# The first phase of a concatenated S4D and attention kernel on one Trainium2 core: its instructions in the order of a list scheduler, seeds of 544 columns, negated factors made in the loop, scaling by dt inside the transposing matmuls

## The chip, the core and the metric

The kernel runs on one core of a Trainium2 chip. The core has five engines with a queue of instructions each: TensorE (PE in the profile; PEld is its load of the stationary operand), VectorE (DVE), ScalarE (ACT), GpSimd (POOL) and SyncE (SP), which here issues nearly all transfers between the device's memory, SBUF and back. Matmuls write to PSUM, of which the kernel uses eight banks of 128 x 512 float32. An engine executes its queue in order; an instruction waits until the semaphores it names have been raised.

The metric is the device time of one execution in microseconds (us). The kernel before takes 1304.7 us, the median of three runs (1302.42 to 1306.85).

## The reference

Two results stand side by side in the output, 2048 x 448 each, in float32.

The first is a diagonal state-space layer (S4D) with D = 448 channels and N = 256 states: its kernel is a sum of 256 complex exponentials, which is then convolved with the input by FFT.

```python
dt = jnp.exp(log_dt)
A = -jnp.exp(log_A_real) + 1j * A_imag
C = (C_real + 1j * C_imag) * dt[:, None]
P = jnp.exp((A * dt[:, None])[:, :, None] * pos[None, None, :])
K = 2.0 * jnp.einsum("dn,dnl->dl", C, P).real
...
y = jnp.fft.irfft(Uf * Kf[None, :, :], L2)[:, :, :L]
return y + u * D_skip[None, None, :]
```

The second is softmax attention with 16 heads of 28 over 2048 positions.

```python
qkv = (x @ wqkv).reshape(B, S, 3, H, Dh)
scores = jnp.einsum("bhqd,bhkd->bhqk", q, k) * Dh ** -0.5
o = jnp.einsum("bhqk,bhkd->bhqd", softmax(scores), v)
return o.transpose(...).reshape(B, S, D) @ wo
```

## The kernel before

`body` has a first phase, a loop and a tail.

**First phase** (the block `with ExitStack() as st`). Two kinds of work run beside each other.

*Projections.* The input x is worked on in four chunks of 512 positions. `transposes` turns a chunk on PE (64 transposes in all) and splits it into a high part `xh` (ACT) and a low part `xl` (DVE). The weights are split in the same way into `w_g` (for queries and keys, kept in the tile that later holds the first keys, `k0_t`) and `vh`, `vl` (for values); ACT makes the high parts, DVE the low parts of `w_g`, POOL those of the values. `qk_proj` makes the queries (s = 0) or keys (s = 1) of one of four head groups for one chunk with 12 matmuls of 512 columns; `v_proj` makes the values of 128 positions with 12 matmuls of 448 columns. In all that is 32 x 12 and 16 x 12 matmuls. The function `evac` that each of them returns splits a result into `hl` (two buffers), by ACT and DVE, and SP stores it to memory (`k_d`, `q_d`, `v_d`); for the first two chunks of keys a difference of two halves, `kd_d`, is stored as well. `project` emits one projection and, behind it, the `evac` of the one before.

*Seeds.* The exponentials are not computed one by one. For each of eight groups of 56 channels, `seeds` makes a few powers of each state's factor (exponentials and sines on ACT, phases reduced on DVE, products on POOL), from which the loop later builds all others by doubling. A group's seeds are 672 columns: 256 for `e` (eight powers of it, the 0th being the constants 1 and 0), 128 for `g` and 288 for `F_Z`, six factors in three forms, namely real part, negated imaginary part and imaginary part. `times_dt` scales four inputs by dt on ACT, then `turn` transposes them on PE. SP stores the seeds to `sd_d` in two parts (`put_e`, `put_g`).

The work is listed in 41 slots (`n_stage`): projections are spread over the first `PW` = 37, the stages of the seeds follow at an offset per group, and `ahead` puts early loads at given slots (`A0`, `A1`, `KW`). In this phase `nc.kept` is empty, and the framework's own scheduler sets the order of the instructions on each engine.

*The first maxima.* The softmax subtracts the exact maximum of each row. One unit of the attention is one head group and one chunk of queries; there are 16 units. For unit 0 the maxima over all keys are made at the end of the first phase, after all projections: the pools of the projections are closed, `load_k(0, j, ...)` has brought the four heads' keys (khat, 16 loads of 256 KB; they lie where the weights lay), and 16 groups of five matmuls follow, with one Relu of 1024 columns on ACT and one combined add and maximum of 1024 columns on DVE per group. `max_end` turns the result and `max_put` stores it into the queries' tile with two small transfers issued by ACT. The loop's first scores need it.

**Loop** (256 steps, `NS`). From here on the written order is kept on all engines. A step handles 128 keys of one unit: four score matmuls (`s_mm`, results `pss`, three banks) whose exponential ACT writes to `p`, four matmuls `po<-p,v`, and four matmuls (`pm`) that prepare the next unit's maxima with DVE's reductions. Between them the step takes pieces of the S4D part: `k_seeds` copies the seeds of one of 56 blocks of eight channels from the loaded tile `sdb` into `e` and `g` on ACT, `e_power` doubles `e` with nine products and sums on POOL, `g_powers` does the same for `g` on DVE from a copy `zg` of the factors (`k_start`), `k_mm` multiplies both on PE, and other jobs (`u_stage1`, `u_stage2`, `spectrum`, `finish`) do the transforms. A block is due every `KP` = 3.5 steps.

**Tail.** After the last blocks, the rest of the spectra, the last unit and the output projection.

Matmuls of float32 operands show in the profile as two or four instructions each; queries, keys and projections use a one-pass type and show as one. All instructions that are issued through the wrapper class `Kept` carry one line number, L76, so groups are told apart by their tiles.

Of the kernel before, what the change touches and what calls it, by code (L numbers as in the profile page):

```python
# [8 lines left out]
F32 = mybir.dt.float32  # L9
# [8 lines left out]
L = 2048  # L18
# [25 lines left out]
A0, A1, KW = 26, 34, (33, 35, 36)  # L44
# [13 lines left out]
F_G = 256  # L58
F_Z = F_G + 128
SDF = F_Z + 18 * 16  # L60
# [5 lines left out]
class Kept:  # L66
# [5 lines left out]
    def __getattr__(self, name):  # L72
        f = getattr(self.engine, name)

        def call(*args, **kw):
            i = f(*args, **kw)  # L76
            return self.owner.tc.keep_in_program_order(i) if self.name in self.owner.kept else i
# [3 lines left out]
class Engines:  # L81
    def __init__(self, tc):
        self.tc, self.kept = tc, ()
# [4 lines left out]
KEPT = {"p": (), "a": ("tensor", "vector", "scalar", "gpsimd", "sync"), "f": ()}  # L88
# [3 lines left out]
def body(ctx, tc, a, out):  # L92
# [41 lines left out]
    k0_p = pool(k0_st, "k0_p", side="right")  # L134
    k0_t = k0_p.tile([128, HG, L], F32R, name="khat")
# [10 lines left out]
    def load_k(g, j, p):  # L146
        if j == 0:
            t = k0_t if g == 0 else p.tile([128, HG, L], F32R, name="khat")
            kt_g[g] = [t[:, i] for i in range(HG)]
# [49 lines left out]
    def max_end(u, ps):  # L199
        nc.tensor.transpose(ps[:16, :128], m_u[u, 1], ident)  # L200
        mh = q_p.tile([16, 2, 128], F32R, name="mh")
# [11 lines left out]
    with ExitStack() as st:  # L213
        sst, xst, wst, mst, psx, psm = (ExitStack() for _ in range(6))
# [3 lines left out]
        y_p = pool(wst, "y_p", side="right")  # L218
        ps_w[0] = pool(psx, "ps_w", 1, PSUM)
# [3 lines left out]

        xns = {}

        def load_x(c):
            xs = x[c * CQ:(c + 1) * CQ, :].rearrange("(t p) d -> p t d", p=128)
            for h in range(2):
                xns[c, h] = y_p.tile([128, 2, D], F32, name="xn", bufs=3)
# [3 lines left out]
        w_g = k0_t[:CK].rearrange("p g (i s k h e) -> p i s k g h e", i=2, s=2, k=NCK, h=HG)  # L233
        vh = y_p.tile([CK, NCK, D], F32R, name="vh")
        vl = y_p.tile([CK, NCK, D], F32R, name="vl")
        nc.gpsimd.memset(k0_t[:CK].rearrange("p g (n e) -> p (g n) e", e=32)[:, :, DH:].bitcast(F32), 0.0)
        vst = [v_p.tile([128, NK // NQ, HG, 32], F32, name="v", bufs=5).rearrange("p t h e -> p (t h) e") for _ in range(2)]
        for t in vst:
            nc.gpsimd.memset(t[:, :, DH:DH + 1], 1.0)
            nc.gpsimd.memset(t[:, :, DH + 1:], 0.0)  # L240
        wns = []
        for i in range(2):
            wn = t_p.tile([128, 3, LV, BO * 16], F32, name="tri", bufs=2).rearrange("p t k h -> p (t k h)")
# [9 lines left out]
        def load_nat(o):  # L253
            nats[o] = s_p.tile([PO, 4, 256], F32, name="nat", bufs=2)
# [4 lines left out]
        dt_all = s_p.tile([PO, 5, NO], F32, name="dt_all")  # L259
# [12 lines left out]
        for k in range(NCK):  # L272
            for s in (1, 0):
# [3 lines left out]
                nc.vector.tensor_tensor(lo, src, hi.bitcast(F32), ALU.subtract)  # L277
# [27 lines left out]
        def turn_dt():  # L305
            dt_ps = ps_t.tile([128, CQ], F32, name="pt")[:PO, :NO]
            nc.tensor.transpose(dt_ps, dt_o, ident[:NO, :NO])
            for i, f in enumerate((1.0, 0.15915494309189535, 2.0, -2.0, -1.0)):
                nc.vector.tensor_scalar(dt_all[:, i, :], dt_ps, f, None, op0=ALU.mult)

# [3 lines left out]
        def seeds(o):  # L314
# [9 lines left out]
            def times_dt(i):  # L324
# [833 lines left out]
```

## Time and profile before

| | |
|---|---|
| median of three runs | 1304.7 us |
| profiled execution, device time | 1307.74 us |
| its span, first to last instruction | 1305.7 us |
| PE busy in the span | 1228.7 us (94%), 12193 matmul instructions |
| DVE, ACT, POOL busy | 907.0 us (69%), 980.3 us (75%), 865.9 us (66%) |
| moved by DMA | 205.28 MB, mean 157 GB/s |
| mean granted TensorE clock | 0.976 |

The profiled execution is one run of its own; its device time is about 2 us above its span and 3.0 us above the median of the three.

A row of a table by stretch gives the stretch, its length, the busy time and number of instructions of PE, PEld, DVE, ACT and POOL, the granted TensorE clock as a share of full speed, the mean busy share of the 16 DMA engines and the rate in GB/s. A row of a group gives line, engine, operation, output tile and input tiles, shapes and count, then busy time and the mean duration in ns, then the idle time of the engine just ahead of these instructions and what ended it. A row of the timeline gives start and duration. Matmuls overlap one another in the records: one of 0.40 us can follow the last after 0.23 us.

### The profile page before, as it was taken

What the parts mean: (1) busy time and instruction counts of PE and PEld (TensorE: products, weight loads), DVE (VectorE), ACT (ScalarE), POOL (GpSimd) and SP (SyncE); (2) the same over time, 40 slices, a digit from 0 to 9 for tenths busy, and PEclk for the clock granted to TensorE, in tenths of its full rate; (3) what the DMA queues carried; (4) which work ended last, traced back from release to release, by engine and by line L of the source; (5) the groups of instructions that cost most, each with busy time, mean ns of one, the idle gap of its engine ahead of it and who ended that gap; (6) DMA issues with size and microseconds to landing.
All of it is one profiled execution on the core that took longest, in us unless ns stands there. A gap on an engine that the chain in (4) does not pass through costs nothing.

```text
span 1305.7 us, 32148 instructions
## 1 busy us (share of the span) xinstructions
PE 1228.7 (94%) x12193; PEld 695.7 (53%) x12193; DVE 907.0 (69%) x2001; ACT 980.3 (75%) x2046; POOL 865.9 (66%) x684
## 2 busy tenths in 40 slices
PE   6888877799999999999999999999997999999998
PEld 5766755355555555555555555555554555545333
DVE  5676656677777787777788888888986555636111
ACT  4877875588888888888788888888886666756463
POOL 2677654478888788888769999999995221424421
PEclk9989887799999999999999999999999999999999
DMA  6677679735866455468634232743324453647666
GB/s 202 207 273 257 218 259 271 212 66 136 185 147 142 109 149 157 142 169 231 162 104 105 56 83 62 157 111 78 82 59 139 146 158 136 203 142 238 202 161 175
DMA packets 200082, 205.28 MB, mean 157 GB/s; under 512 B 95992, under 2 KB 158520, under 8 KB 197880
## 3 DMA queue, kind: packets, MB, share of 16 engines
q1 hardware_dynamic: 199864, 203.22, 56.1%
q8 instruction: 96, 1.57, 0.5%
q14 instruction: 58, 0.48, 0.1%
q10 hardware_dynamic: 64, 0.02, 0.0%
HBM read 120.74 MB, written 82.18 MB: 155 GB/s over the span
## 4 chain that ended last, share of the span: by engine, by line
PE 72%; POOL 8%; ACT 7%; DVE 5%; DMA 4%; issue 4%; SPq 0%; ACTq 0%; POOLq 0%
PE pm L76 39%; PE pss L76 16%; PE po L76 16%; POOL sg L76 2%; POOL e L76 2%; DMA khat<-k 2%; POOL tri L76 2%; ACT tri L76 1%; ACT sg L76 1%; DVE mx L76 1%; POOL p L76 1%; ACT L76 1%; ACT p L76 1%; POOL eu L76 1%; DVE rl L76 1%
## 5 line engine op out<-in xcount | busy, mean ns | idle before, releaser
L76 ACT ACTIVATE p<-pss 128x512 f32<-128x512 f32 x1024 | 560.4, 609 | 109.9 <-PE pss L76 105.9
L76 PE MATMUL pss<-qhat,khat 128*128 128x512 f32 x1024 | 405.7, 402 | 4.0 <-DMA qhat<-mh 2.2
L76 DVE TENSOR_REDUCE mx<-pm 128x1 f32<-128x512 f32 x480 | 308.3, 683 | 121.2 <-PE pm L76 119.5
L76 PE MATMUL pm<-khat,qhat 128*128 128x512 f32 x720 | 314.4, 437 | 6.1 <-ACT rl L76 3.5
L76 POOL TENSOR_TENSOR e<-e,sdb 128x256 f32<-128x256 f32 x168 | 202.0, 1203 | 108.7 <-ACT e L76 67.2
L76 PE MATMUL po<-p,v 128*32 128x512 f32 x2048 | 271.0, 597 | 0.0
L76 POOL TENSOR_TENSOR e<-e,eu 128x256 f32<-128x256 f32 x168 | 248.3, 1478 | 13.2
L76 PEld LDWEIGHTS pm<-khat,qhat 128*128 128x128 f32 x720 | 135.4, 188 | 206.4 <-ACT p L76 47.0
L76 PEld LDWEIGHTS pss<-qhat,khat 128*128 128x128 f32 x1024 | 191.2, 189 | 52.5 <-ACT p L76 13.8
L76 DVE CUSTOM_DVE_ANT_0 rl<-pm,rl 128x512 f32<-128x512 f32 x240 | 165.3, 689 | 70.0 <-ACT rl L76 67.7
L76 POOL TENSOR_TENSOR eu<-e,sdb 128x256 f32<-128x256 f32 x168 | 202.3, 1204 | 0.0
L76 POOL TENSOR_TENSOR p<-pr,pr 64x448 f32<-64x448 f32 x64 | 73.2, 1144 | 155.6 <-PE pm L76 122.3
L76 DVE TENSOR_TENSOR g<-g,zg 128x128 f32<-128x128 f32 x392 | 162.0, 413 | 3.6
L76 ACT ACTIVATE rl<-pm 128x512 f32<-128x512 f32 x240 | 145.3, 605 | 7.7 <-issue 4.1
L76 PE MATMUL pm<-xh,khat 112*128 112x512 f32 x256 | 89.7, 431 | 19.6 <-DVE hl L76 10.6
L76 PE MATMUL pm<-kdif,qhat 128*128 128x512 f32 x240 | 97.0, 404 | 1.7 <-DVE pr L76 1.1
L76 DVE TENSOR_TENSOR zg<-g,zg 128x128 f32<-128x128 f32 x224 | 88.0, 393 | 5.3
L76 PEld LDWEIGHTS pm<-e,g 128*32 128x32 f32 x3584 | 56.9, 110 | 49.2 <-issue 15.7
L76 PE MATMUL pm<-e,g 128*32 128x64 f32 x3584 | 73.6, 223 | 8.7 <-POOL e L76 8.7
L76 ACT ACTIVATE y<-pm 128x448 f32<-128x448 f32 x48 | 26.5, 553 | 59.7 <-PE pm L76 39.1
L76 PEld LDWEIGHTS pm<-xh,khat 112*128 112x128 f32 x256 | 51.0, 205 | 35.9 <-DVE hl L76 12.6
L76 DVE TENSOR_TENSOR pr<-pm,ub 128x448 f32<-128x448 f32 x64 | 37.0, 619 | 46.9 <-PE pm L76 37.7
(133 smaller groups left out, 1491.6 us busy)
## 6 DMA issues: line engine op xcount, KB each, us to landing
sdb<-sd SPq DMA_DIRECT2D x56, 336.0 KB
khat<-k SPq DMA_DIRECT2D x64, 256.0 KB
qhat<-q SPq DMA_DIRECT2D x64, 256.0 KB
sd<-sg SPq DMA_DIRECT2D x8, 1456.0 KB
k<-hl SPq DMA_DIRECT2D x16, 512.0 KB
q<-hl SPq DMA_DIRECT2D x16, 512.0 KB
v<-v SPq DMA_DIRECT2D x32, 256.0 KB
mw<-in_mw SPq DMA_DIRECT2D x16, 512.0 KB
```

Of the source, the lines that this page charges most:

```text
L76: i = f(*args, **kw)
```

## The change

- **Order of the first phase.** The instructions of the phase are no longer emitted at once but collected by a new class `Plan`, each with an assumed duration, the tiles it reads and writes and a tag (p for projections, s for seeds, m for maxima). `Plan.order` is a list scheduler: it computes for each instruction the longest chain behind it, and then repeatedly takes, for the engine that is free first, the ready instruction with the longest chain (chains of seeds are weighted). The instructions are emitted in that order, which is then kept on all five engines. So that the plan can tell buffers apart, the tiles of a ring are allocated once and taken in turn (`ring`).
- **First maxima inside the phase.** The groups of unit 0 are part of the plan. The weights move to a tile of their own, so that the first keys' tile takes the place of the values' weights and the input's tiles (`change`), and is loaded once those are done. The last chunk's work starts with the keys of head group 0, then its four value projections, then the other seven projections. Each group's work is in two halves of 512 columns: 32 Relus and 32 combined maxima. The projections get three buffers of one pool (`pm_r`), shared with the maxima.
- **Splitting the weights.** The low parts of `w_g` are made on POOL instead of DVE.
- **Seeds of 544 columns.** The 0th power of `e` is no longer stored (224 columns), but set once in the loop's two `e` tiles; of the three forms of a factor, two are stored (192 columns). In the loop ACT makes the negated form of 96 columns for each of the 56 blocks, into the tail of `sdb`; the products read the two imaginary forms in reverse order.
- **Scaling by dt.** Three of the four inputs are no longer scaled by ACT; instead their transposes become matmuls with an identity scaled by dt (`dg`, made once on POOL). The factor 2 moves into the constant `wb`.
- **Smaller edits.** One exponential over all 15 powers in place of two instructions; one copy of `g` in place of four; a negation in `g_base` moves from ACT to POOL.

The diff, cut to its core:

```diff
-A0, A1, KW = 26, 34, (33, 35, 36)
+A0, A1 = 18, 28
+MG = {41: (2, ()), 42: (3, ()), 43: (0, (8, 9)), 44: (1, (10, 11)), 45: (None, (12, 13)), 46: (None, (14, 15)), 47: (None, (0, 1)),
+      48: (None, (2, 3)), 49: (None, (4, 5)), 50: (None, (6, 7))}
-F_G = 256
+F_G = 14 * 16
 F_Z = F_G + 128
-SDF = F_Z + 18 * 16
+SDF = F_Z + 12 * 16
+SDN = SDF + 6 * 16
...
+            if self.owner.plan is not None:
+                return self.owner.plan.add(self.name, name, f, args, kw)
...
-KEPT = {"p": (), ...
+KEPT = {"p": ("tensor", "vector", "scalar", "gpsimd", "sync"), ...
...
+    def order(self):
+        for o in reversed(self.ops):
+            k = o.tag, o.engine
+            tail[o.i] = max([cost(o) + self.GAP + tail[j] for j in after[o.i]] + [o.span + chain.get(k, 0.0), cost(o)])
...
+        while len(out) < n:
+            e = min((e for e in pools if pools[e]), key=lambda e: max(free[e], min(ready[i] for i in pools[e])))
+            t = max(free[e], min(ready[i] for i in pools[e]))
+            best = max((i for i in pools[e] if ready[i] <= t + 1e-9),
+                       key=lambda i: tail[i] * self.SCALE[self.ops[i].tag] + self.BIAS[self.ops[i].tag] - ...)
...
-                nc.vector.tensor_tensor(lo, src, hi.bitcast(F32), ALU.subtract)
+                nc.gpsimd.tensor_tensor(lo, src, hi.bitcast(F32), ALU.subtract)
...
+            for i in range(2):
+                nc.gpsimd.tensor_tensor(dg[:, i], ident[:PO, None, :PO].to_broadcast([PO, NO, PO]),
+                                        dt_all[:, i, :, None].to_broadcast([PO, NO, PO]), ALU.mult)
...
-                        nc.tensor.transpose(ps[:, i, :, h, :], q["nat"][:, i, h * 128:(h + 1) * 128], ident[:PO, :PO])
+                        if i == 1:
+                            nc.tensor.transpose(ps[:, i, :, h, :], n, ident[:PO, :PO])
+                        else:
+                            nc.tensor.matmul(ps[:, i, :, h, :], n, dg[:, int(i != 2), o].rearrange("p (b e) -> p b e", e=8), start=True, stop=True)
...
-            jobs = v_jobs + jobs if c == NQ - 1 else jobs + v_jobs
+            jobs = jobs[:1] + v_jobs + jobs[1:] if c == NQ - 1 else jobs + v_jobs
...
+        def max_group(i):
+            for h in range(2):
+                pd, pb = pt_r(), pm_r()
+                if h == 0:
+                    mm(pd, q, kd_g[0, j], start=True, stop=True)
+                    mm(pb.rearrange("p (c n) -> p c n", c=2), q, k_late(j, CQ, ...), start=True, stop=True)
+                else:
+                    mm(pd, q, quarter(2), start=True, stop=False)
+                    mm(pd, Late(("nq", j), 128, lambda: nqs[j][:, ts]), quarter(3), start=False, stop=True)
+                    mm(pb, q, quarter(3), start=True, stop=True)
+                rl = rl_r()
+                nc.scalar.activation(rl, pd, AF.Relu)
+                nc.vector.tensor_tensor_reduce(rl, pb, rl, 1.0, -3.0e38, ALU.add, ALU.max, m_u[0][:, j, t, h:h + 1])
...
+        nc.plan = None
+        plan.run()
...
-            es[b] = e = g_p.tile([128, 2, 16, N2], F32, name="e", bufs=2)
-            nc.scalar.activation(e[:, :, :, :8], sds[b][:, :F_G].rearrange("p (c e h) -> p c h e", c=2, e=8), AF.Copy)
+            es[b] = e = e_t[b % 2]
+            nc.scalar.activation(e[:, :, :, 1:8], sds[b][:, :F_G].rearrange("p (c e h) -> p c h e", c=2, e=7), AF.Copy)
+            nc.scalar.activation(sds[b][:, SDF:], sds[b][:, SDF - 96:SDF], AF.Copy, scale=-1.0)
```

More of the change, by code (lines that the diff above doesn't have):

```diff
@@ L213, in body @@
     with ExitStack() as st:
-        sst, xst, wst, mst, psx, psm = (ExitStack() for _ in range(6))
+        sst, xst, wst, yst, psx = (ExitStack() for _ in range(5))
+        k0 = []
         t_p = pool(sst, "t_p")
@@ L505, in body @@
         slots[1].insert(0, turn_dt)
-        pend, n_work = [], len(work)
+        n_work = len(work)
         ahead = collections.defaultdict(list)
```

392 lines of the change are left out of this document (280 added, 112 removed).

## The prediction

> **What bounds the kernel now.** I read the table of busy time by stretch first, to see where an engine is short of work.
>
> ```profile
> 0.00:40.00 40.00, 29.07 (x125) 21.51 (x125) 24.38 (x54) 21.52 (x45) 11.96 (x24) 1.00 0.64 194
> 40.00:180.00 140.00, 122.64 (x544) 97.52 (x544) 93.68 (x139) 107.78 (x183) 97.21 (x67) 0.94 0.74 249
> 180.00:243.00 63.00, 39.87 (x123) 27.18 (x123) 37.12 (x64) 34.07 (x44) 20.83 (x17) 0.77 0.92 262
> 243.00:650.00 407.00, 402.90 (x4497) 215.75 (x4500) 315.61 (x746) 341.32 (x770) 332.41 (x261) 0.99 0.60 150
> 650.00:980.00 330.00, 326.95 (x3803) 183.29 (x3795) 287.52 (x688) 285.10 (x636) 302.01 (x237) 1.00 0.38 91
> 980.00:1306.00 326.00, 307.31 (x3111) 150.49 (x3111) 148.69 (x313) 190.49 (x371) 101.47 (x81) 0.99 0.56 170
> ```
>
> After the stretch and its length come busy time and instructions of PE, PEld, DVE, ACT and POOL, then the granted clock, the DMA share and GB/s. From 243 us on PE is busy 99% of the time up to 980: the attention loop is PE's. Up to 243 us, the first phase, no engine is full, and PE least of all at its end: 544 matmuls in 140 us (3.9 per us), then 123 in 63 us (2.0 per us). So the change is decided in the first phase, and above all after 180 us. The chain of waits there, in order of time:
>
> ```profile
> 208.44 9.86 DMA khat<-k
> 218.32 10.46 DMA khat<-k
> ...
> 236.38 5.56 DMA qhat<-mh
> ```
>
> Two loads of the first keys hold the end for 20 us, then come the last maxima and the 5.56 us store of the maxima into the queries. PE in that stretch, by group, and single rows of the timeline (start, duration):
>
> ```profile
> L76 PE MATMUL p<-khat,qhat 128*128 128x512 f32 x48 | 19.2, 466 | 1.2 <-DMA khat<-k 1.2
> L76 PE MATMUL pm<-xh,khat 112*128 112x512 f32 x24 | 10.4, 524 | 8.0 <-DVE hl L76 8.0
> L76 PE MATMUL p<-kdif,qhat 128*128 128x512 f32 x16 | 7.6, 473 | 7.8 <-DVE hl L76 7.1 <-ACT rl L76 0.7
> L76 PE MATMUL p<-khat,nq 128*128 128x512 f32 x16 | 7.1, 454 | 0.0
> L76 PE MATMUL pm<-xl,khat 112*128 112x512 f32 x12 | 6.1, 504 | 0.0
> ```
> ```profile
> 191.22 0.39 PE L76 MATMUL pm<-xl,khat 112*128 112x512 f32 x1
> ...
> 191.92 0.40 PE L76 MATMUL pm<-xl,khat 112*128 112x512 f32 x1
> ...
> 195.75 0.73 PE L76 MATMUL pm<-xh,khat 112*128 112x512 f32 x2 [2.73 <-DVE hl L76]
> ...
> 197.51 0.63 PE L76 MATMUL pm<-xl,khat 112*128 112x512 f32 x1
> ...
> 198.79 0.63 PE L76 MATMUL pm<-xl,khat 112*128 112x512 f32 x1
> ...
> 233.28 0.73 PE L76 MATMUL p<-khat,qhat 128*128 128x512 f32 x2
> ...
> 242.89 0.77 PE L76 MATMUL pss<-qhat,khat 128*128 128x512 f32 x1 [2.18 <-DMA qhat<-mh]
> ```
>
> Three projections (36 matmuls) and the 80 matmuls of the first unit's maxima run here. From one xl row to the next lie three matmuls: 0.70 us before the gap at 195.75, so 0.233 us each, and 1.28 us after it, so 0.427. At 0.233 the 116 matmuls are 27 us of work in a stretch of 63. PE ends the last maximum at 234.0; the loop's first scores (pss) start at 242.89, 8.9 us later.
>
> **The change part by part.** *The order.* The last chunk's keys of head group 0 are now projected first, then its values, and the first keys' 16 loads stand in SP's queue among the last seven projections' stores. The 80 matmuls stand between those projections on PE. All five engines follow one written order. The 16 loads of kd, four of q and four of the second unit's q also move ahead of stores on SP. So the question is at what rate PE gets through what is left. I count from 40 us. Of the 544 + 123 matmuls, about 6 belong to the loop already: 661. At the middle stretch's 140/544 = 0.257 us each that is 170 us. The later ones are longer than the middle's mean, which holds 88 small transposes, here by group for 40 to 180 us:
>
> ```profile
> L76 PE MATMUL pt<-ident,xn 128*112 128x128 f32 x40 | 6.0, 279 | 1.9 <-DVE xl L76 1.9
> L76 PE MATMUL pn<-ident,nat 56*128 56x56 f32 x48 | 4.2, 228 | 0.0
> ```
>
> If these cost nothing, a middle matmul would be 456/544 x 0.233 = 0.195 us of full-rate work, if they cost as much as the others 0.233; I take 0.203. For the end's 116 at 0.233 that adds 116 x 0.03 x 0.257/0.203 = 4 us, so 174 us, at a granted clock of 0.94. If the gaps that cost clock go, 174 x 0.94 = 164. Bounds: the whole stretch as it ran before, 234 - 40 = 194 us, and 661 x 0.208 (545 at 0.203, 116 at 0.233) at full rate without a gap, 138 us; with 5% gaps 145. I take 163, near the one with full clock, because the order fills the waits for hl (8.0 and 7.1 us above) with other matmuls.
>
> The Trainium skill, "TensorE: Matmul & The Clock Gate", Part 1, says that PE falls to half clock after an idle window of about 3.4 us and needs such a window of work to come back. Our row agrees nearly: after 2.73 us of recorded waiting the matmuls took 0.427 us until 199.2. By that rule alone, 8 scattered gaps of this size would cost 8 x 1.7 = 14 us more than the gaps themselves, and the 163 would be about 175 again.
>
> *Splitting the weights.* Eight subtractions move from DVE to POOL.
>
> ```profile
> L76 POOL TENSOR_TENSOR vl<-tri,vh 112x448 fp32r<-112x448 f32 x4 | 5.1, 1279 | 12.7 <-ACT vh L76 9.4 <-DMA pw<-in_pw 3.2
> 16.85 4.13 DVE L76 TENSOR_TENSOR khat<-tri,khat 112x448 fp32r<-112x448 f32 x4
> ```
>
> POOL then does 12 at 1.28 us in a row, 15.3 us from about 10 us on, so 25.3; before, DVE had the last at 21.0. The first complete projection waits up to 4.3 us; PE has two more banks to work in, so between 0 and 4.3. I take 3.
>
> *Smaller seeds and scaling in the matmul.* ACT loses 24 of 32 scalings, POOL eight negations.
>
> ```profile
> L76 ACT ACTIVATE nat<-nat,dt_all 56x256 f32<-56x256 f32 x32 | 14.7, 498 | 3.7 <-DVE dt_all L76 3.3 <-DMA nat<-in_A_C_imag 0.3
> L76 POOL TENSOR_SCALAR sg<-sg 128x672 f32<-128x672 f32 x8 | 16.7, 2090 | 0.6
> DMA packets 42954, 59.06 MB, mean 243 GB/s; under 512 B 3032, under 2 KB 31736, under 8 KB 42427
> 220.00:240.00 20.00, 14.76 (x56) 9.05 (x54) 14.87 (x29) 11.07 (x12) 0.00 (x0) 0.93 1.05 292
> ```
>
> That is 24 x 0.498 = 12.0 us off ACT and 16.7 off POOL. POOL gets back eight weight parts (10.2) and eight small negations (0.7 each at the 672 columns' rate, 5.6), so it stays near 129. ACT falls from 163 to about 150, less by the merged copies. Neither is full in 214 us, so both are worth nothing by themselves: PE's work covers them. The maxima in halves change 16 ACT and 16 DVE instructions into 32 each; DVE stays near 155, 73% of 214. The transposes that scale are 48 matmuls in place of 48 transposes of the same shape; I cost them at nothing, bounded by their neighbours, 0 to 48 x 0.1 us. Of DMA, each of eight stores of seeds falls by 7 x 128 x 128 columns x 4 bytes, 3.7 MB in all: 59.06 - 3.7 - 1.0 (three loads that belong to the loop) = 54.4 MB, at the 292 GB/s of the 220:240 stretch 186 us. It must be spread well to fit, but fits. The saving is worth between 0, if packets count, and 3.7/0.292 = 12.7 us; I take 0, since PE ends later.
>
> *Sum of the phase.* 40 + 3 + 163 + 8.9 = 215 for the first scores, against 242.9: 28 us earlier.
>
> *Negated factors in the loop.* 56 more ACT instructions of 96 columns; the seeds' copy falls from 256 to 224.
>
> ```profile
> L76 ACT ACTIVATE p<-pss 128x512 f32<-128x512 f32 x766 | 420.0, 610 | 49.4 <-PE pss L76 47.2 <-PE pm L76 1.2
> L76 ACT ACTIVATE e<-sdb 128x256 f32<-128x256 f32 x56 | 37.6, 671 | 6.0 <-DMA sdb<-sd 6.0
> L76 ACT ACTIVATE zg<-sdb 128x144 f32<-128x144 f32 x55 | 17.0, 309 | 10.5 <-DVE g L76 9.7
> POOL e L76 <- ACT e L76: 6.2, 5, 2.1
> ```
>
> A copy of 96 columns takes at most zg's 0.309 us (144 columns) and at least two thirds of it, 0.206; I take 0.28: 15.7 us, less 56 x 0.671 x 32/256 = 4.7 from the shorter copy: 11 us more (7 to 13) in a loop where ACT waits 47 us for PE's scores. Queued behind it are the next p copies, which PE's next scores wait for through three banks, and on POOL the e powers. POOL is 302 of 330 us busy from 650 us, and waited for ACT's e only five times there (last row), so at most a few of the 0.28 us reach it. Of that between 0 and 13 comes out; I take 2. Reading the factors in reverse order adds no instruction; the shorter loads of seeds are hidden, as DMA is at 38 to 60% there.
>
> *Total.* -28 + 2 = -26. The profiled span of 1305.7 becomes 1279.7, its device time of 1307.74 becomes 1281.7. That execution stood 3.0 above the median of 1304.7, so I forecast 1304.7 - 26 = 1279, rounded.
>
> **The rivals.** *Packed to the floor.* With 5% gaps and no late start PE needs 145 us: first scores at 40 + 145 + 8.9 = 194, 49 us earlier. DMA's 186 us would just allow it. For it: all waits on PE in the middle are short. Against: in the middle DVE, POOL, DMA, ACT and PE are already 67% to 88% busy. Time 1304.7 - 49 + 2 = 1258.
>
> *Transfers set the phase.* If DMA keeps the phase's mean of 243 GB/s, 54.4 MB take 224 us; the last keys land some 8 us before that, as q, v and seeds come after, then 5 us of maxima and 8.9: first scores at 230. For it: the share of 0.92 after 180 us. Against: 292 GB/s was reached there. Time 1304.7 - 13 + 2 = 1294.
>
> *The loop pays.* If all 11 us of ACT come out, and 27 blocks x 0.28 = 8 us more through POOL's late powers, 28 - 19 = 9 remain: 1296. Against it: ACT's 47 us of waiting.
>
> *The other side, slower: the stores behind the first keys' loads.* Place: SP's queue, where the stores of the last seven projections stand among 16 loads of 256 KB. A projection's result has two hl buffers; if its store waits behind a load that itself waits for PE, ACT and DVE stop, PE's three banks fill, and the loads' maxima stand behind them in PE's queue. For it: the hl waits in the rows of PE. Price: the last 164 matmuls (7 x 12 + 80, 38.3 us of work) run at the rate r of full that the end had before, 27/63 = 0.43, or somewhat better, 0.5. The matmuls before them, 138 - 38.3 = 99.3 us, at the middle's 0.203/0.257 = 0.79, take 126: with r = 0.5, first scores at 40 + 3 + 126 + 77 + 8.9 = 255, 12 us later, 1304.7 + 12 + 2 = 1319. It decides from r = 0.57 down, where the time is 3.9 above the median.
>
> *It doesn't do what it says.* If the order only reshuffles, as every engine ran in one order before too, the 194 us stay: 1304.7 + 3 + 2 = 1310.
>
> **How the numbers follow.** The forecast, 1279 with its own range of 1268 to 1289, 0.52; packed 0.14; transfers 0.13; the loop 0.08; slower 0.10; nothing gained 0.03. The range reaches to the packed case and past the loop's: 1256 to 1300. What can be told from no change is 0.3%, 3.9 us: faster is below 1300.8, which holds the first four cases, 0.87 less 0.02 for their upper ends, so 0.85; slower is above 1308.6: 0.10, most of the slower case and half of the last; the rest, 0.05, is the same.
>
> **What would show it.** The first pss at 215, at 0.84 of full rate on PE from 40 us, with the last seven projections between rows of the maxima; khat loads that end before the last projection; the granted clock of the middle at 0.98 or more; ACT some 11 us busier in the loop and its wait for pss shorter by as much, with PE still at 99%. The forecast is wrong if PE waits for hl or for khat more than 10 us after 180, if DMA stands at its full share before the keys land, or if the loop from first pss to the end, 1305.7 - 242.9 = 1062.8 us now, comes out over 1067.

## The result and the profile after

The changed kernel takes 1342.0 us (median of four runs, 1341.3 to 1342.9). The kernel before, on the same chip, takes 1304.9 (1302.4 to 1306.9). The ratio is 1.0286, with a 95% interval of 1.0267 to 1.0304: slower by 2.9%, where 1279 us was forecast. The profiled execution has a span of 1340.1 us.

The busy time by stretch of the changed kernel, with the columns of the table shown before:

```profile
0.00:40.00 40.00, 28.87 (x121) 22.58 (x122) 18.41 (x43) 18.61 (x37) 22.05 (x27) 0.94 0.62 183
40.00:180.00 140.00, 103.21 (x428) 81.58 (x427) 96.62 (x133) 91.18 (x123) 92.46 (x63) 0.82 0.66 215
180.00:243.00 63.00, 53.93 (x216) 42.39 (x215) 26.70 (x51) 26.79 (x41) 17.28 (x12) 0.90 0.81 232
243.00:650.00 407.00, 394.73 (x4166) 211.88 (x4167) 307.87 (x732) 328.89 (x753) 304.15 (x244) 0.98 0.55 137
```

The middle stretch is where it goes wrong: 428 PE instructions in 140 us where there were 544, at a granted clock of 0.82 where it was 0.94. ACT and POOL are busy less there too (91 us for 108, 92 for 97), in part because the change took work off both. So no engine has become the bound; they wait for one another. Single rows of the timeline (start, duration) of the changed kernel, from several engines, in order of time:

```profile
35.24 5.96 POOL L171 TENSOR_TENSOR tri<-tr,pw 128x1680 f32<-128x1680 f32 x2 [5.00 <-ACT tr L171]
...
41.16 2.39 POOL L171 TENSOR_TENSOR dhl<-kb,dhl 128x256 fp32r<-128x256 f32 x1
...
43.59 0.38 ACT L171 ACTIVATE kb<-pm 128x256 f32<-128x256 f32 x1 [3.38 <-POOL dhl L171]
...
48.02 1.61 POOL L171 TENSOR_TENSOR sg<-tri,sg 128x672 f32<-128x672 f32 x1 [4.46 <-ACT sg L171]
...
55.92 0.99 DVE L171 TENSOR_TENSOR sg<-pn,tri 128x224 f32<-128x224 f32 x2 [4.53 <-POOL tri L171]
...
59.51 0.40 DVE L171 TENSOR_TENSOR px<-pn,tri 128x224 f32<-128x224 f32 x1
...
59.96 1.95 PE L171 MATMUL pn<-dg,nat 56*128 56x56 f32 x8 [10.79 <-DVE px L171]
...
63.53 0.38 ACT L171 ACTIVATE kb<-pm 128x256 f32<-128x256 f32 x1 [5.99 <-POOL dhl L171]
...
67.50 1.22 PE L171 MATMUL pm<-xh,w 112*128 112x512 f32 x2 [5.58 <-DVE hl L171]
68.51 0.63 PE L171 MATMUL pm<-v,w 112*128 112x512 f32 x1
68.94 1.05 PE L171 MATMUL pm<-xh,w 112*128 112x512 f32 x2
...
275.57 0.37 PE L171 MATMUL pt<-ident,m 128*16 128x128 f32 x1 [1.82 <-DVE m L171]
...
279.54 0.63 PE L81 MATMUL pss<-qhat,khat 128*128 128x512 f32 x1
```

PE stands for 10.79 us at the scaling matmuls of a group of seeds, since both buffers of pn are still read by DVE for earlier groups; the read that frees one ends at 59.91. DVE had itself waited 4.53 us for POOL, and POOL 4.46 us for ACT before that. ACT had stood 3.38 us for `dhl`, the low part of a difference of keys, which POOL made only after the size products of two groups in a row (5.96 us). Everything behind these instructions in the queues of PE and ACT waits with them: ACT stands 5.99 us more for the next `dhl`, and PE 5.58 us for an `hl` whose ACT part comes behind it. How many projections stood ready in PE's queue isn't shown. The first scores come at 279.54 us, 36.7 later than before (242.89). From there to the end it is 1340.1 - 279.5 = 1060.6 us, against 1062.8. So the whole loss, and more, is in the first phase.

### The profile page after: what moved, and what is told of

It is laid out like the page before. It is cut to its first block, busy times and chain, and to the rows that moved or that the text cites. A ratio compares the mean times of both kernels' runs of the same rounds, so it can differ in the third digit from the quotient of the medians.

```text
span 1340.1 us, 32401 instructions
## 1 busy us (share of the span) xinstructions
PE 1249.2 (93%) x12241; PEld 709.9 (53%) x12241; DVE 913.5 (68%) x2024; ACT 974.7 (73%) x2054; POOL 868.3 (65%) x682
## 4 chain that ended last, share of the span: by engine, by line
PE 76%; DVE 4%; ACT 4%; POOL 3%; issue 3%; DMA 1%; ACTq 0%; SPq 0%; DVEq 0%; POOLq 0%
PE pm L81 39%; PE pss L81 17%; PE po L81 16%; PE pm L171 4%; ACT p L81 1%; POOL tri L171 1%; POOL p L81 1%; DVE mx L81 1%; PE pt L171 1%; POOL e L81 1%; ACT rl L171 1%; DVE rl L171 0%; DVE zg L81 0%; DVE rl L81 0%; DMA q<-hl 0%
## 5 line engine op out<-in xcount | busy, mean ns | idle before, releaser
L171 PE MATMUL pm<-xh,w 112*128 112x512 f32 x256 | 90.5, 440 | 11.9 <-DVE hl L171 7.5
L81 ACT ACTIVATE y<-pm 128x448 f32<-128x448 f32 x48 | 26.5, 553 | 59.5 <-PE pm L81 35.7
L81 PEld LDWEIGHTS po<-p,v 128*32 128x32 f32 x2048 | 54.1, 110 | 26.2 <-issue 21.6
```

The lines of the kernel that those rows point to most:

```text
L171: f(*[x_.fn() if isinstance(x_, Late) else x_ for x_ in args], **{k: x_.fn() if isinstance(x_, Late) else x_ for k, x_ in kw.items()})
```

## The experiments

The description of the change says that the list's order is then kept on all five engines. The code doesn't do that:

```python
            if self.owner.plan is not None:
                return self.owner.plan.add(self.name, name, f, args, kw)
            i = f(*args, **kw)
            return self.owner.tc.keep_in_program_order(i) if self.name in self.owner.kept else i
```

While a plan is open, the call returns in the second line, having handed the engine's bare method `f` to the plan. `Plan.run` later calls `f`, and the pin of the last line is never made, although `KEPT["p"]` names all engines. So the list orders the program's text, and the framework's scheduler orders each engine once more. The rows above show it: two size products (tri<-tr,pw) in a row, ahead of `dhl`.

### Who orders the phase

Four kernels: the plan with its order pinned; the operations in the order of the listing, not pinned; the same, pinned; and the pinned plan without favour for the seeds.

```diff
-            f(*[x_.fn() if isinstance(x_, Late) else x_ for x_ in args],
-              **{k: x_.fn() if isinstance(x_, Late) else x_ for k, x_ in kw.items()})
+            self.keep(f(*[x_.fn() if isinstance(x_, Late) else x_ for x_ in args],
+              **{k: x_.fn() if isinstance(x_, Late) else x_ for k, x_ in kw.items()}))
...
-        plan = nc.plan = Plan()
+        plan = nc.plan = Plan(); plan.keep = tc.keep_in_program_order
```

> The changed kernel with one addition: each instruction that the plan replays is pinned behind the one before it on its engine, so that the written list is the order on all five engines. In the changed kernel the list only sets the order of the program text, and the framework orders each engine's instructions once more. Theory A (the written order never reached the engines, and the second ordering put seeds ahead of what projections wait for): the first pss moves from 279.5 us to 215-235, the time to 1275-1300, and PE's wait of 10.8 us for DVE px near 60 us goes. Theory B (the list itself is bad, since it is made from assumed durations with no slack and favours seeds): the first pss stays at 270 or later, the time at 1330-1350 or above. Theory C (dearer single operations, such as two-SBUF products on DVE at 0.94 us and twice the PE instructions for scaling): first pss at 260-280 in any order.

```diff
-        for i in self.order():
+        for i in range(len(self.ops)):
```

> The changed kernel, but the plan replays its operations in the order in which they were listed, and nothing is pinned: the framework alone orders the phase, as in the kernel before. All other edits stay. Theory A (second ordering of an already reordered list is what costs): the framework does with the listing about what it did before, first pss at 235-255, time 1297-1318. Theory B (the list itself is bad): the same 1297-1318, so this run separates both from C. Theory C (dearer single operations): first pss at 260-280, time 1325-1345, much as in the changed kernel.

> The changed kernel with the operations replayed in listing order and pinned: no reordering by anyone. It says what any reordering is worth. Theory A: slower than the pinned plan by 10-60 us, since the listing lets each engine stand at waits: first pss at 240-290. Theory B: the listing interleaves seeds by hand-set stages, so it is better than the plan's order: first pss at 225-250. Theory C: 260-280 again.

```diff
-    SCALE = {"p": 1.0, "s": 1.6, "m": 1.0, "d": 1.0}
-    BIAS = {"p": 0.0, "s": 20.0, "m": 0.0, "d": 0.0}
+    SCALE = {"p": 1.0, "s": 1.0, "m": 1.0, "d": 1.0}
+    BIAS = {"p": 0.0, "s": 0.0, "m": 0.0, "d": 0.0}
```

> The pinned plan with the seeds no longer favoured (their rank times 1.0 plus 0 in place of times 1.6 plus 20). Theory A: the favour is a choice made for the pinned order, so within 10 us of the pinned plan, either side. Theory B (favoured seeds make PE, ACT and POOL stand at seed work): 15-40 us faster than the pinned plan. Theory C: the same as the pinned plan, 260-280.

| kernel | median, us | ratio to before (95%) | first pss, us |
|---|---|---|---|
| before | 1303.4 | | 242.9 |
| plan, pinned | 1303.2 | 0.9998 (0.9986 to 1.0010) | 239.6 |
| listing, not pinned | 1336.5 | 1.0247 (1.0228 to 1.0266) | 269.4 |
| listing, pinned | 1440.5 | 1.1049 (1.1033 to 1.1066) | 376.1 |
| plan, pinned, seeds not favoured | 1307.6 | 1.0028 (1.0016 to 1.0039) | 246.1 |

The pin alone brings 40 us: the first scores move from 279.5 to 239.6. The pinned plan, by stretch and in single rows of the timeline:

```profile
0.00:40.00 40.00, 25.82 (x92) 19.32 (x92) 17.21 (x40) 16.20 (x33) 20.94 (x27) 0.91 0.61 182
40.00:180.00 140.00, 121.52 (x541) 98.80 (x542) 110.34 (x153) 100.65 (x138) 100.49 (x66) 0.89 0.74 243
180.00:243.00 63.00, 55.57 (x217) 39.81 (x216) 39.74 (x91) 30.44 (x56) 13.25 (x16) 0.96 0.90 259
```
```profile
34.60 3.00 POOL L171 TENSOR_TENSOR tri<-tr,pw 128x1680 f32<-128x1680 f32 x1 [4.96 <-ACT tr L171]
37.55 0.74 POOL L171 TENSOR_TENSOR dhl<-kb,dhl 128x256 fp32r<-128x256 f32 x1
41.95 3.01 POOL L171 TENSOR_TENSOR tri<-tr,pw 128x1680 f32<-128x1680 f32 x1 [3.66 <-ACT tr L171]
...
235.68 0.27 PE L171 MATMUL pt<-ident,m 128*16 128x128 f32 x1 [1.51 <-DVE m L171]
...
239.60 0.63 PE L81 MATMUL pss<-qhat,khat 128*128 128x512 f32 x1
```

Now `dhl` stands between the two size products, as the list has it, and 541 PE instructions fit into the middle. Theory A is right in kind, but its numbers were missed by a little (239.6 for 215 to 235, 1303.2 for 1275 to 1300; PE's longest wait for px is still 7.8 us): the pinned plan is no faster than the kernel before, so something else of the change costs time, or the list isn't good. Theory C, 260 to 280 in any order, falls by the same row. Of theory B the favour for the seeds falls: without any, the first scores come 6.5 us later, where 15 to 40 us faster was expected. That a list made from assumed durations is itself poor stays open here. The listing with a pin missed the ranges of all three theories: 376.1 us, 137 later than the pinned plan. So a pin is worth what its order is worth: it won 40 us on the computed order and lost 107 on the listing (376.1 for 269.4).

The listing without a pin comes out at 269.4, where theory C has it and theory A (235 to 255) doesn't. So with the framework's order alone, as in the kernel before, the other edits of the change already cost 26.5 us, and the list's text, ordered once more, 10.1 on top. Its rows show no dear single operation but a queue. The timeline of that kernel:

```profile
200.06 0.57 ACT L171 ACTIVATE sg<-pn 128x224 f32<-128x224 f32 x1 [6.06 <-DVE px L171]
200.65 1.28 ACT L171 ACT_TABLE_LOAD   x1
202.78 1.04 ACT L171 ACTIVATE tri<-tri 128x1008 f32<-128x1008 f32 x1 [0.85 <-DVE tri L171]
203.73 0.58 ACT L171 ACTIVATE rl<-pt 128x512 f32<-128x512 f32 x1
204.36 0.80 PE L171 MATMUL pt<-kdif,qhat 128*128 128x512 f32 x1 [13.48 <-ACT rl L171]
```

PE stands 13.48 us at a first maximum, because the Relu (rl) of the one before stands on ACT behind the copies and sines of the last seeds. In the kernel before the maxima came after all seeds. This one wait is half as long as the 26.5 us. That it cost as much isn't shown: the granted clock was 0.50 as well from 243 us to the first scores of this kernel. The rows speak for it that the maxima inside the phase need an order that is held.

### Single operations of the change

The pinned plan, with one edit undone in each of three kernels and all three in a fourth. Each was listed anew.

```diff
-                for k, src, e in ((0, c0, 1), (1, c0, 2), (1, g4_(1), 3)):
+                for k, src, e, dst in ((0, c0, 1, c1), (1, c0, 2, g4_(2)), (1, c1, 3, g4_(3))):
...
-                    tt(g4_(e), g4_(e), x_, ALU.add)
+                    tt(dst, g4_(e), x_, ALU.add)
...
+                act.activation(q["g4"][:, :, :, :, 1], q["c1"].rearrange("p c b h -> p b c h"), AF.Copy)
```

> The pinned plan, with the intermediate product of the seeds kept in PSUM as before (c1 in px, and eight ACT copies put it in its place), so that no DVE product has two SBUF inputs. In the pinned plan these 16 products took 13.5 + 7.1 us, single ones up to 5.33 us while POOL ran three operations back to back; with a PSUM input they took 0.57 and 0.40 us, 7.7 us for 16. Theory D (such products stand until POOL's running work ends, and PE then stands at the scaling matmuls behind them): first pss moves from 239.6 to 226-234, the time to 1287-1297. Theory P (PE sets the phase by its clock and its number of instructions, and DVE's late products are covered): 236-243, time 1300-1307.

```diff
-                n = q["nat"][:, 1, :]
-                act.activation(n, n, AF.Copy, scale=dt_all[:, 2, o:o + 1])
+                for i, f in ((1, 2), (2, 0), (3, 1)):
+                    act.activation(q["nat"][:, i, :], q["nat"][:, i, :], AF.Copy, scale=dt_all[:, f, o:o + 1])
...
+                act.activation(q["nat"][:, 0, :], q["nat"][:, 0, :], AF.Copy, scale=dt_all[:, 1, o:o + 1])
...
-                        if i == 1:
+                        if True:
```

> The pinned plan, with the scaling by dt back on ACT (32 ACT instructions, eight there already) and plain transposes in place of the scaling matmuls, as before. The scaling costs PE 96 instructions of 0.33 us in the records where transposes were 48 of 0.23. Theory P (the small scaling matmuls cost PE twice the instructions and let its clock fall): first pss 226-235, time 1287-1298. Theory D: DVE and POOL are untouched, ACT gets 12 us more: 238-246, time 1299-1310. Prediction's price of nothing: 239 and 1303.

```diff
-                nc.gpsimd.tensor_tensor(lo, src, hi.bitcast(F32), ALU.subtract)
+                nc.vector.tensor_tensor(lo, src, hi.bitcast(F32), ALU.subtract)
```

> The pinned plan, with the eight low parts of the weights back on DVE, as before. On POOL they kept DVE's first small operations waiting (1.07 us in place of 0.18 us, three times) and put off the seeds of the first group. If the late front carries through (the pinned plan has 92 matmuls by 40 us, the kernel before 125): first pss 4 to 8 us earlier, 231-236, time 1295-1299. If it is made up later: 237-241, time 1301-1305. The prediction priced the move at 3 us.

> The pinned plan with all three undone: PSUM products, scaling on ACT, weights on DVE. What is left of the change is the order, the maxima between the projections, the smaller seeds and the negation in the loop. If the single operations are what kept the pinned plan from the forecast of 215: first pss 212-226, time 1273-1289. If it is the plan's assumption of a full clock and no slack: 230-240, time 1294-1304.

| kernel | median, us | ratio to before (95%) | first pss, us |
|---|---|---|---|
| product of the seeds in PSUM | 1311.5 | 1.0061 (1.0043 to 1.0078) | 251.4 |
| scaling on ACT | 1304.8 | 1.0007 (0.9995 to 1.0018) | 241.6 |
| weights on DVE | 1301.4 | 0.9987 (0.9974 to 1.0001) | 239.7 |
| all three | 1299.4 | 0.9967 (0.9954 to 0.9980) | 237.6 |

None of the gains that undoing an edit was to bring came, and one kernel lost 12 us. Three came out where the other theory had them: the scaling at 241.6 (238 to 246), the weights at 239.7 (237 to 241), all three at 237.6 (230 to 240). The product in PSUM fits neither of its ranges. These runs are inconclusive about the operations: a change of one operation gives another list, and the list can weigh more. The product in PSUM came out at 251.4 here; with the old list held, and with a second sum on DVE in place of ACT's copies, it comes out at 235.9 (below). How much of the 15.5 us is the list and how much the copies wasn't separated. What is learnt is how to ask: hold the list.

### The same list, and a list that knows of a wait

In the pinned plan the rows of DVE show something the list knows nothing of. Its products by group, up to 240 us:

```profile
L171 DVE TENSOR_TENSOR sg<-sg,px 128x224 f32<-128x224 f32 x24 | 13.7, 572 | 0.7
L171 DVE TENSOR_TENSOR sg<-sg,tri 128x224 f32<-128x224 f32 x8 | 13.5, 1685 | 0.0
L171 DVE TENSOR_TENSOR px<-pn,tri 128x224 f32<-128x224 f32 x16 | 6.7, 417 | 1.5 <-POOL tri L171 0.6 <-PE pn L171 0.4 <-ACT tr L171 0.3
L171 DVE TENSOR_TENSOR px<-sg,tri 128x224 f32<-128x224 f32 x8 | 7.1, 884 | 0.0
```

With one input in PSUM (px, pn) a product of 224 columns takes 0.57 or 0.42 us; with both in SBUF (sg and tri) the means are 1.69 and 0.88. Of these 16 products twelve took 0.54 to 0.92 us and four 2.28 to 5.33 us, so a few long ones make the difference. Single rows of the timeline of the same kernel show what the longest stood behind:

```profile
18.36 2.26 POOL L171 TENSOR_TENSOR w<-tri,w 112x448 fp32r<-112x448 f32 x2
18.48 1.07 DVE L171 TENSOR_SCALAR kf<-x 8x56 f32<-8x56 f32 x1
...
183.59 3.73 POOL L171 TENSOR_TENSOR qhat<-tri 128x784 f32<-128x784 f32 x2
185.61 5.33 DVE L171 TENSOR_TENSOR sg<-sg,tri 128x224 f32<-128x224 f32 x1
187.28 3.25 POOL L171 TENSOR_TENSOR sg<-tri,sg 128x672 f32<-128x672 f32 x2
```

The DVE product that begins at 185.61 ends at 190.94, just behind POOL's last one (190.53). The tiny 8x56 operation at 18.48 ends about when the first of two POOL operations does (half of their 2.26 us behind 18.36, so 19.49), and takes 1.07 us; in the kernel before, the same took a sixth of that:

```profile
21.11 0.18 DVE L76 TENSOR_SCALAR kf<-x 8x56 f32<-8x56 f32 x1
```

The Trainium skill, "SBUF — State Buffer", section "Who interferes with whom", says that a DVE instruction with two SBUF inputs contends with a GpSimd instruction that reads SBUF, that the ports they share are an exclusive lock, and that the order of issue decides who blocks. The trace agrees that such a product can stand until POOL is done (190.94 for 190.53), but not in the order: the product also stood behind two POOL operations that began after it, from 187.28 on. The change moved work to the wrong side of that rule: the seeds' product now has both inputs in SBUF (`g4_(1)` in place of px). It also put the weights' subtractions on POOL, beside DVE's first operations. The tiny one among these has a single SBUF input, so this rule doesn't cover it; that it waited is what its row shows.

To price these without a new list, the pinned plan's own order was written out as numbers, and one thing changed in it. For the PSUM product DVE makes the sum twice, once for PSUM and once for its place.

```diff
-        for i in self.order():
+        for i in self.written():
...
-                for k, src, e in ((0, c0, 1), (1, c0, 2), (1, g4_(1), 3)):
+                for k, src, e in ((0, c0, 1), (1, c0, 2), (1, c1, 3)):
...
+                    if e == 1:
+                        tt(c1, g4_(e), x_, ALU.add)
+                        plan.extra.add(len(plan.ops))
                     tt(g4_(e), g4_(e), x_, ALU.add)
```

> The pinned plan with its own order written out, so that nothing is listed anew; only the seeds' intermediate product goes to PSUM, and DVE makes it twice, once for PSUM and once for its place (eight more DVE operations of 0.57 us). No DVE product of the seeds has two SBUF inputs then. Theory L (a DVE operation whose operands all lie in SBUF stands until POOL's running operations end): the 20.6 us of those 16 products become 7.7, plus 4.6 for the added ones, and PE's waits for DVE px (8.9 us) shrink: first pss 228-235 in place of 239.6, time 1289-1296. Theory R (the former trial with PSUM was slower because PE sets the phase, by its count and its clock): 237-243, time 1300-1307.

The second takes the same written order, and the one line that moves the weights' low parts to DVE.

> The pinned plan with its own order written out; only the eight low parts of the weights go back to DVE, at the same places of the list. Theory L: DVE's first small operations no longer stand behind POOL's (1.07 us in place of 0.18), the seeds of the first group come 3 us earlier, and more of PE's matmuls lie before 40 us (92 in the pinned plan, 102 when it was listed anew): first pss 234-238. Theory R: what is won at the front is lost again at the first group's seeds, since POOL and ACT set these: 238-241.

The third is listed anew, with both moves (the product in PSUM made twice, the weights on DVE), a milder favour, and one rule more in the list:

```diff
-    SCALE = {"p": 1.0, "s": 1.6, "m": 1.0, "d": 1.0}
-    BIAS = {"p": 0.0, "s": 20.0, "m": 0.0, "d": 0.0}
+    SCALE = {"p": 1.0, "s": 1.2, "m": 1.0, "d": 1.0}
+    BIAS = {"p": 0.0, "s": 10.0, "m": 0.0, "d": 0.0}
...
+        o.alone = engine == "vector" and not any(isinstance(x_, Late) or x_.space == PSUM for x_ in aps)
...
                 t += self.TABLE
+            if o.alone:
+                t = max(t, free["gpsimd"])
```

> The pinned plan, listed anew with three edits: the seeds' product in PSUM as in the run before, weights on DVE, and a list that knows of the wait: a DVE operation with all operands in SBUF is placed behind the end of POOL's last placed operation. The seeds' favour is 1.2 and 10 in place of 1.6 and 20. Theory L: the list now tells where DVE will stand, so it holds on the chip: first pss 205-222, time 1266-1283, and the granted clock of the middle rises from 0.89 to 0.95 or more. Theory R: the list is as far off as before: 232-245, time 1293-1306.

The fourth leaves that rule out again (without the lines with `o.alone`).

> The same as the run before but for the list's knowledge of DVE's wait behind POOL, which is left out; the favour of the seeds is 1.2 and 10 here too. Theory L: 8 to 25 us later than the run that knows of it: first pss 218-240. If the milder favour and the two moves alone do it: within 5 us of that run. Theory R: 232-245, as that run.

| kernel | median, us | ratio to before (95%) | first pss, us |
|---|---|---|---|
| same list, product in PSUM | 1296.3 | 0.9945 (0.9924 to 0.9967) | 235.9 |
| same list, weights on DVE | 1300.6 | 0.9972 (0.9958 to 0.9986) | 239.0 |
| list that knows of the wait | 1281.6 | 0.9825 (0.9810 to 0.9840) | 219.6 |
| the same without that rule | 1291.7 | 0.9896 (0.9876 to 0.9915) | 229.9 |

With the list held, the product in PSUM brings 3.7 us by the first scores of one profile each, which falls between theory L's range and theory R's and is nearer to L's; by the ratios to before (0.9945 for 0.9998) it brings 6.9. The weights bring 0.6 by the first scores and 3.4 by the ratios. PE has 100 instructions behind it at 40 us in place of 92, and then stands 7.7 us for px near 56 us as in the pinned plan: most of the head start is lost again, as theory R had it.

The list with the rule is 10.3 us ahead of the one without, as theory L had it, and its kernel is the best: 1281.6 us, inside L's range. That the rule works by the wait it tells of isn't shown. These are two new lists, and one operation's change moved a new list by 12 us above. Nor does DVE stand less with the rule. Its large products with both inputs in SBUF, the only ones left in the seeds, with the rule (first row) and without:

```profile
L172 DVE TENSOR_TENSOR tri<-tri 128x1680 f32<-128x1680 f32 x8 | 17.3, 2158 | 0.2
L171 DVE TENSOR_TENSOR tri<-tri 128x1680 f32<-128x1680 f32 x8 | 16.1, 2006 | 0.1
```

Of the 20.0 us between the pinned plan and the best kernel, 3.7, 0.6 and 10.3 make 14.6. The other 5.4 come with the milder favour and the new listing together. The best kernel by stretch and at its first scores (one line was added above, so L171 is L172 there):

```profile
0.00:40.00 40.00, 29.88 (x110) 22.89 (x111) 18.91 (x47) 17.18 (x34) 9.52 (x18) 0.96 0.78 227
40.00:180.00 140.00, 130.87 (x605) 107.24 (x604) 109.34 (x163) 102.11 (x145) 101.83 (x67) 0.92 0.81 258
180.00:243.00 63.00, 56.86 (x290) 34.02 (x292) 51.14 (x133) 40.34 (x78) 33.59 (x30) 0.97 0.70 204
```
```profile
215.66 0.27 PE L172 MATMUL pt<-ident,m 128*16 128x128 f32 x1 [1.51 <-DVE m L172]
...
219.59 0.63 PE L81 MATMUL pss<-qhat,khat 128*128 128x512 f32 x1
```

605 PE instructions fit into the middle, 61 more than in the kernel before; the scaling, which shows as 48 more over the whole phase, accounts for a part of them. The clock there reaches 0.92, not the expected 0.95.

### Two questions left

Was the missing pin a mishap of one list? And does scaling in the matmuls cost time once the list holds? The first kernel is the best one without the pin, the second the best one with the scaling back on ACT.

> The kernel with the list that knows of DVE's wait behind POOL (first pss 219.6, 1281.6 us), with the pin taken away: the list only orders the text, and the framework orders each engine again, as in the changed kernel. If the missing pin is the cause for any list: first pss 240-285, time 1301-1347. If the 40 us were a mishap of the one list of the changed kernel: 217-232, time 1279-1294.

> The pinned kernel with the list that knows of DVE's wait, and the scaling by dt back on ACT with plain transposes (48 fewer PE instructions, 24 more on ACT, listed anew). If the scaling in the matmuls costs PE what the records say, 96 x 0.277 - 48 x 0.228 = 15.6 us of busy time, and PE sets the phase now: first pss 206-216, time 1268-1278. If it costs nothing, as the prediction had it: 217-222. If ACT's added 12 us decide: 222-232, time 1284-1294.

Without the pin: 1343.9 us, ratio 1.0303 (1.0286 to 1.0320), first scores at 283.3. The best list tried, ordered once more by the framework, ends where the changed kernel did; the pin is worth 62 us there. Its middle:

```profile
40.00:180.00 140.00, 112.87 (x463) 89.67 (x462) 84.30 (x126) 82.33 (x117) 81.11 (x57) 0.82 0.60 201
```

With the scaling on ACT: 1283.6 us, ratio 0.9851 (0.9830 to 0.9873), first scores at 220.6. The two groups of the scaling kernel, and the one that takes their place:

```profile
L172 PE MATMUL pn<-dg,nat 56*128 56x56 f32 x96 | 13.4, 277 | 1.4 <-DVE tri L172 1.2 <-DVE pn L172 0.2
L172 PE MATMUL pn<-ident,nat 56*128 56x56 f32 x16 | 2.6, 231 | 4.4 <-DVE tri L172 4.4
```
```profile
L172 PE MATMUL pn<-ident,nat 56*128 56x56 f32 x64 | 7.3, 236 | 4.7 <-ACT dhl L172 2.7 <-DVE tri L172 2.0
```

PE is relieved of 13.4 + 2.6 - 7.3 = 8.7 us, ACT gets 24 scalings more, and the first scores move by 1.0 us, the other way. So no cost of the scaling shows here; as two lists can differ by 12 us, a small one isn't excluded.

## Why the prediction was wrong

**The step that failed** is the 163 us for what PE has left from 40 us on, taken "because the order fills the waits for hl with other matmuls", and under it the sentence that all five engines follow one written order. Nothing made the engines follow it, and POOL's rows show that it didn't. With the 3 us of a late start the prediction has 166 us from 40 us to PE's last maximum. PE's last work before the scores (pt<-ident,m, right behind the maxima) began at 275.57 in the changed kernel, 235.6 us after 40. With the pin it began at 235.68, so 195.7 us; with the pin and the best list at 215.66, so 175.7. The step's value can be approached, then, but not by what the change does; and the held order alone, which is what was forecast, gave 195.7, no better than the kernel before (235.71, also 195.7).

**Its count was too low as well.** 661 matmuls were counted, which is right for the kernel before. The groups of PE in the pinned plan add up to 834 instructions of the phase, and 834 - 110 = 724 were left at 40 us in the best kernel. 48 of the difference of 63 are the scaling matmuls: each of the 48 shows as two instructions (x96), where a transpose shows as one. The other 15 are work that the kernel before had done by 40 us (125 instructions for 110). The rate that was forecast, 163/661 = 0.247 us per instruction, was missed by the changed kernel: 834 - 121 = 713 were left, so 235.6/713 = 0.330. The best kernel reached 175.7/724 = 0.243; that this is so near is in part luck, since the 48 instructions more are short ones.

**The 8.9 us** from the last maximum to the first scores were too high: in the best kernel only 3.9 us lie between the turn of the maxima at 215.66 and the scores, where the same two rows lay 7.2 us apart before (235.71 and 242.89).

**What the prediction didn't see** is the move of the seeds' product from PSUM to SBUF inputs: neither the sum nor a rival has it. With the list held, its undoing brought 3.7 us by the first scores. A new list made with the wait in it was 10.3 ahead of one without, for a cause that stays open.

**The clock.** The paragraph on scattered gaps warned of 14 us. It went that way: after the gap of 5.58 us the matmuls stand 0.43 us apart (68.51 and 68.94), and the middle had 0.82 of full clock. PE from 40 us to the first scores, before and in the changed kernel, with the granted clock behind the count:

```profile
40.00:242.80 202.80, 162.39 (x666) 0.89 0.79 253
40.00:279.50 239.50, 183.65 (x720) 0.85 0.66 207
```

PE stands 55.9 us in place of 40.4, 15.5 more; the other 21 us of the loss it is recorded as busy. The lower clock and the 54 more instructions share these 21, and how they share them wasn't separated.

**Costed about right.** Splitting the weights on POOL, 3 us taken and 0 to 4.3 given: 0.6 by the first scores and 3.4 by the ratios with the list held. Scaling in the matmuls at nothing: no cost showed, though only between new lists. The halves of the maxima at nothing: no run has them alone. The loop, +2 of 0 to 13: it came out 2.2 shorter (1060.6 for 1062.8), though ACT got more than was expected. ACT's rows from 243 us on in the changed kernel:

```profile
L81 ACT ACTIVATE e<-sdb 128x224 f32<-128x224 f32 x56 | 34.9, 622 | 0.0
L81 ACT ACTIVATE sdb<-sdb 128x96 f32<-128x96 f32 x56 | 17.1, 306 | 0.0
```

17.1 us were added (15.7 forecast) and the copy of `e` fell by 2.7, from 37.6 to 34.9 (4.7 forecast). That is 14.4 more, beyond the 7 to 13, and none of it shows in the loop's length.

**The rivals.** The slower one put the stall into SP's queue, among the first keys' loads after 180 us. It isn't there: PE's waits for khat are not among its waits after 180, and for hl it waits 0.6 us there. The stall is on POOL, DVE and ACT, from seeds, and mostly earlier: by 180 us PE had done 549 instructions, where it had done 669 before. "It doesn't do what it says" had the right condition, at 0.03, but priced it at 194 us of PE as before; an order that is shuffled once more can be worse than none, as the two unpinned plans (37 and 40 us later than before) show beside the listing (26.5 us later). Two of the prediction's signs of failure, waits for hl or khat of more than 10 us after 180 and a loop over 1067, didn't appear though it failed: they watched the end of the phase and the loop, not whether the list was followed.

## What to carry to other kernels

An order that is computed must be looked for in the trace, engine by engine, before its worth is argued: here one wrapper call that wasn't reached was worth 40 and 62 us. A list made from durations doesn't know which engines block one another; here a list that was told came out 10.3 us ahead, in one pair of lists, and why stays open. To price one operation under such a list, hold the list: a new one can move the time by as much as the operation, or more.

## What the runs showed of the hardware

A DVE product with both inputs in SBUF stood 5.33 us behind three POOL operations in turn, not only behind the one that ran when it began. It works the other way too: in the changed kernel POOL's `dhl` took 2.39 us at 41.16, and 0.74 in the pinned plan. It met a DVE operation of the same kind:

```profile
39.46 3.51 DVE L171 TENSOR_TENSOR tri<-tri 128x1680 f32<-128x1680 f32 x1
```

POOL's products ended at 41.20, this one at 42.97, `dhl` at 43.55: the times fit that DVE stood until 41.20 and `dhl` until 42.97.

The clock fell without a marked gap. Three stretches of 2 us each of the changed kernel:

```profile
32.00:34.00 2.00, 2.00 (x20) 1.76 (x19) 1.41 (x2) 0.23 (x1) 0.00 (x0) 1.00 0.03 6
34.00:36.00 2.00, 1.90 (x12) 1.65 (x11) 0.16 (x1) 1.28 (x4) 0.76 (x1) 0.80 0.09 23
36.00:38.00 2.00, 2.00 (x7) 1.70 (x7) 1.08 (x2) 1.22 (x4) 2.00 (x1) 0.50 0.18 57
```

From 31.49 to 36.67 PE's rows hold nothing but small scaling matmuls (56 x 56) and transposes, PE is recorded as busy all but 0.1 us of the first two stretches, and yet the granted clock falls to 0.5 from about 35 us, and stays there until 42. Nothing was tried to tell whether it was these small matmuls.
